# Attention and routed experts on one core: k'q's sixth step of batch 1 in routing step 5, a step's squares between slot 0's casts and joins, step 3's scatters behind slot 0's rows

## The chip, the cores and the metric

The kernel runs on one core of one Trainium2 chip. The metric is the device time of one execution in microseconds (us); for the kernel before it is the median of three runs. The profile is of one more execution, taken by the hardware profiler.

## What is computed

Channel attention over four batches, and a mixture of experts on its output. Cut to what matters:

```python
B, N, C = 4, 5056, 256                      # q, k, v: [B, N, C] float32
qn = q / (norm(q, axis=1) + 1e-6)           # norms over the N tokens
kn = k / (norm(k, axis=1) + 1e-6)
a  = softmax(kn^T @ qn / tau)               # per batch [C, C]
x  = (v @ a).reshape(20224, 256)
logits = x @ w_gate + modality_bias[modality_id]     # 8 experts
e = argmax(logits); g = softmax(logits)[e]
out[t] = g[t] * (relu(x[t] @ w1[e]) @ w2[e])         # w1: 256x1024, w2: 1024x256
```

## The kernel before

**Steps.** Tokens are taken 512 at a time: ten steps per batch, the last one short. Three kinds of work run over such steps.

- *k'q* (`kq_pieces(b, s)`): q and k of the step are loaded (L302), their product is added to the 256x256 matrix `g` of the batch on TensorE (L365), and their squares are added to `acc` for the norms: ScalarE squares (`sq`, L344), VectorE adds (L346), two halves of two squares and two adds a step. In batch 0, and in the first six steps of batch 1 (indices 0 to 5, `WHOLE`), the float32 values go to TensorE as they are; later steps are split into a high and a low part first (`qs`, `ks`: ScalarE cast L320, VectorE subtraction L321). Squares can be put off: with a list `later` they are run when the text reaches that list.
- *Routing* (`va_pieces`, `g` counts the steps 0 to 39 over all batches): v of the step is transposed, split into `vh` and `vl` (L571, L572), multiplied by the attention matrix (`xp`, L585), copied to `x` (L592 to L597) with the gate's logits beside it (`L`, L598), and every token gets a row number. GpSimd then scatters the 512 rows to `xs` in DRAM by four indirect DMAs (`send`, L474). For steps 0 to 5 v is transposed by TensorE (`vtp`); from step 6 on by a transposing DMA (`T`, L534) and a second one that takes the half-words apart (`pl`, L511), whose parts ScalarE and VectorE join again (`vt`, L518, L519).
- *Blocks* (`block_pieces`): a slot is a block of 512 rows of one expert. `load_x` fetches its rows with a transposing DMA (`Tx`, L766) and its weights and tokens (`gt`, L769); `load_w` fetches w1 and w2 in halves (`w1r`, `w2r`, L788, L792); `split_w` casts them and subtracts (L811, L818); `tr_x` joins the rows (`xt`, L518, L519) and splits them (`xh`, `xl`, L830, L831); `m1` and `m2` are the two matrix products (`hp` L845, `y` L866) with relu and its low part between them (`hh` L848, `hl` L849); `finish` and `store` scale the result and scatter it to the output.

**Order.** Batch 0's k'q runs first, alone. Then the routing steps follow one another, and the pieces of a step are interleaved with those of a block and with k'q steps of the next batch. `first_block` is 6: slot 0 is computed in routing step 6. It is chosen after step 2 and needs the rows of steps 0 to 2; slot 1 needs step 3's too. `PLAN` says which k'q steps of batch 1 run beside which routing step; `product` makes the pieces of such a task, `ask` issues its load, `products_of` puts both in order. `squares` holds squares put off to the end of a step.

The text is not the order on the engines. A planner takes the instructions of each engine's queue by priority (the place in the text) and by its own estimate of when they are ready, so an instruction can run ahead of its place. `order(ins, others)` keeps an instruction behind others on the same queue without a wait; `after(ins, others)` is a true wait. Each queue then runs strictly in its order. All loads are issued on SyncE's queue (SP), all scatters on GpSimd's (POOL).

`HELD` names routing steps whose scatters are not sent at once: those of steps 3 and 4 were sent in the next step, behind its fourth copy. `turned` is slot 0's `tr_x`, called at the end of step 5 with the instructions behind which its joins are kept, before the change the last cast and subtraction of `split_w` (`evicted[-1]`).

Buffers that matter: `q` and `k` have two each, which indices 0, 1 and 4 onwards of batch 1 use in turn; indices 2 and 3 use the three of `w1r` and `w2r`, which slot 0's weights need next; the `x` of steps 1 and 3 use the two of `Tx`.

Of the kernel before, what the change touches and what calls it, by code (L numbers as in the profile page):

```python
# [13 lines left out]
AF = mybir.ActivationFunctionType  # L14
ALU = mybir.AluOpType
# [20 lines left out]
def kernel(  # L36
# [13 lines left out]
    nc = tc.nc  # L50
    P = 128
    B, N, C = q.shape
# [4 lines left out]
    NS = -(-N // STEP)  # L57
# [19 lines left out]
    START = 2  # L77

    BEFORE = [0, 1]
    PLAN = [[], [2], [], [3], [4], [], [5], [], [6, 7], [8, 9]]  # L80
    AHEAD = 4

    SKIP = (12,)

    first_block = LAG + START

    HELD = {3: 3, 4: 3}

    def parts(s):
        return P if s < NS - 1 else PL  # L90
# [82 lines left out]
    pads = []  # L173
    asked = []
    turning = []
    written = [[] for _ in range(G)]

    def pad_rows():
# [87 lines left out]

    gram = {}
    filled = []
    acc = {}

    def kq_pieces(b, s, behind=(), later=None):

        pp = parts(s)
        st = {}
        t0 = s * STEP

        def act(ins):
            order(ins.ins, [i for n, i in (behind() if callable(behind) else behind) if n == "act"])

        def dve(ins):  # L280
            order(ins.ins, [i for n, i in (behind() if callable(behind) else behind) if n == "dve"])

        def begin():
            if s == 0:
                gram[b] = ps1.tile([P, CH, C], F32, tag="y0" if b == 0 else "g", name=f"g_{b}")
                acc[b] = p1.tile([P, 2, 2 * C], F32, tag="acc", name=f"acc_{b}", bufs=2)
                if b == 0:
                    p1.tile([P, 48], F32, tag="filler2", name="filler2")

        def load():  # L290
            if b == 0:
                begin()
            for n, src, tag in (("q", q, "w1r"), ("k", k, "w2r")):
                if (b == 0 and s % 5 >= 2) or (b == 1 and 2 <= s < START + 2):
                    st[n] = p3.tile([P, TT, C], F32, tag=tag, name=f"{n}_{b}_{s}")
                else:
                    st[n] = p2.tile([P, TT, C], F32, tag=n, name=f"{n}_{b}_{s}")
                rows = src[b, t0 : t0 + pp * TT, :].rearrange("(p t) c -> p t c", t=TT)
                if b == 0 and s == 0:
                    st[n + "rows"] = rows  # L300
                else:
                    nc.sync.dma_start(st[n][:pp], rows)  # L302
            if b == 0 and s == 0:
                for h in range(2):
                    ts = slice(2 * h, 2 * h + 2)
                    for n in ("q", "k"):
                        nc.sync.dma_start(st[n][:, ts, :], st[n + "rows"][:, ts, :])

        def split(h):
            if b > 0 and h == 0:  # L310
                begin()
            ts = slice(2 * h, 2 * h + 2)
            whole = s in WHOLE[b]
            more = h == 1 and (b == 0 or (b == 1 and s < START + 1))
            if not whole:
                st["q", h] = p2.tile([P, 2, 2 * C], F32R, tag="xh" if more else "qs", name=f"qs_{b}_{s}_{h}")
                st["k", h] = p2.tile([P, 2, 2 * C], F32R, tag="xl" if more else "ks", name=f"ks_{b}_{s}_{h}")
            for n in () if whole else ("q", "k"):
                t = st[n, h]
                act(nc.scalar.copy(t[:pp, :, 0:C], st[n][:pp, ts, :]))  # L320
                dve(nc.vector.tensor_tensor(  # L321
                    t[:pp, :, C : 2 * C], st[n][:pp, ts, :], t[:pp, :, 0:C].bitcast(F32), ALU.subtract
                ))
            if later is None:
                square(h)
            else:
                later.append(lambda: square(h))

        def square(h):
            ts = slice(2 * h, 2 * h + 2)  # L330
            a = acc[b]
            for n, o in (("q", 0), ("k", C)):
                first = h == 0 and s == 0
                sq = a[:, :, o : o + C]
                if not first:
                    if b == 0 and s == 0 and n == "q":
                        p3.tile([P, 80], F32, tag="filler5", name="filler5", bufs=1)
                    if b == 0 and n == "k" and not filled:
                        filled.append(p3.tile([P, 48], F32, tag="filler1", name="filler1", bufs=1))
                    if b == 0 or (b == 1 and s < AHEAD):  # L340
                        sq = p3.tile([P, 2, C], F32, tag="hh" if n == "q" else "hl", name=f"sq_{b}_{s}_{h}_{n}")
                    else:
                        sq = p3.tile([P, 2, C], F32, tag="vt", name=f"sq_{b}_{s}_{h}_{n}")
                act(nc.scalar.activation(sq[:pp], st[n][:pp, ts, :], AF.Square))  # L344
                if not first:
                    dve(nc.vector.tensor_tensor(a[:pp, :, o : o + C], a[:pp, :, o : o + C], sq[:pp], ALU.add))  # L346

        def mm(h):
            for t in range(2):
                first = s == 0 and h == 0 and t == 0  # L350
                last = s == NS - 1 and h == 1 and t == 1
                for m in range(CH):
                    ms = slice(m * P, (m + 1) * P)
                    if s in WHOLE[b]:
                        seq = [(st["k"][:pp, 2 * h + t, ms], st["q"][:pp, 2 * h + t, :])]
                    else:
                        ks, qs = st["k", h], st["q", h]
                        lo = slice(C + m * P, C + (m + 1) * P)
                        seq = [
                            (ks[:pp, t, ms], qs[:pp, t, 0:C]),  # L360
                            (ks[:pp, t, ms], qs[:pp, t, C : 2 * C]),
                            (ks[:pp, t, lo], qs[:pp, t, 0:C]),
                        ]
                    for i, (x, y) in enumerate(seq):
                        nc.tensor.matmul(  # L365
                            gram[b][:, m, :], x, y, start=first and m == 0 and i == 0,
                            stop=last and i == len(seq) - 1, skip_group_check=True,
                        )

        yield load  # L370
        for h in range(2):
            yield lambda h=h: split(h)
            yield lambda h=h: mm(h)
# [97 lines left out]
    routed = {}  # L471
# [24 lines left out]
    def lag(g):  # L496

        n = LAG
        for x in SKIP:
            n -= g >= x + n  # L500
        return n
# [245 lines left out]
    def block_pieces(g, slot, picked, tail):  # L747
        pki, padded = picked
        st = {"wr": {}, "wc": {}, "h": {}}
# [11 lines left out]
        def load_x():  # L761
# [3 lines left out]
            for ins in (  # L765
# [10 lines left out]
                        ins.ins, group=f"x{later}", reason="the block's rows were all there when it was taken"  # L776
                    )
                tc.add_to_no_dep_group("xr", ins.ins)
                if slot == 1:
                    turning.append(ins.ins)  # L780

        def load_w(hf):
            if hf == 0:
# [142 lines left out]
    def run(pieces):  # L926
        for f in pieces:
            f()
# [48 lines left out]
    def product(n):  # L977
        g, b, i = tasks[n]
        if n not in products:
            products[n] = list(kq_pieces(  # L980
                b, i, (lambda: routed.get(g, routed[g - 1])) if b == 1 else (),
                squares.setdefault(g + (3 if g + 2 == first_block else 1), [])
                if b == 1 and (g < first_block or i == NS - 1) else None,
            ))
        return products[n]
# [3 lines left out]
    def ask(n):  # L989
        if n < len(tasks) and n not in loaded:  # L990
            loaded.add(n)
            product(n)[0]()

    def products_of(g):

        out = []
        for n, (at, b, i) in enumerate(tasks):
            if at == g:
                out += [lambda n=n: ask(n)] if g <= first_block else []
                out += product(n)[1:]  # L1000
                if g >= first_block and (b, i) != (1, NS - 1):
                    out.append(lambda n=n: ask(n + (1 if g == first_block else 2)))
        if g == first_block + 1:
            out.append(lambda: ask(min(n for n in range(len(tasks)) if tasks[n][0] > g) + 1))
        return out

    va = [va_pieces(*divmod(g, NS)) for g in range(G)]
# [9 lines left out]
    for g in range(G):  # L1017
# [12 lines left out]
            done.add((0, "prep"))  # L1030
            begun = [split0, split1]
        own = list(va[g][1])
        if g - 1 in HELD:
            t = HELD[g - 1]
            own.insert(t + 1, lambda: va[g - 1][4]([copied[g, t]]))
        turn = []
        if g + 1 < first_block:
            turn.append(va[g + 1][2])
# [13 lines left out]
        if b + 1 < B:  # L1052
            if b == 0 and s == 1:
                streams.append(list(kq_pieces(1, 2, lambda: routed[1], squares[2])))
            else:
                streams.append(products_of(g))
        _interleave(*streams)
        if waiting and waiting[0][0] <= g + 1 - lag(g + 1):
            blk = waiting[0][1]
            once(blk, "load")  # L1060
            if blk["slot"] == 0:
                turned(blk["evicted"][-1])
            once(blk, "prep")
        if s == NS // 2 + 2 and b < B - 1:
            setup_bias(b + 1, routed[g])
# [91 lines left out]
```

## Time and profile before

| | |
|---|---|
| median of 3 runs | 1173.28 us (1173.11 to 1174.34) |
| the profiled execution: time, span | 1176.94 us, 1175.1 us |
| granted TensorE clock | 0.998 |
| busy: TensorE, weight loads, VectorE, ScalarE, GpSimd | 1152.9, 1054.9, 919.4, 806.5, 386.9 us |
| DMA | 228.38 MB, mean 194 GB/s |

The span runs from the first to the last instruction. PE is TensorE's matmuls, PEld its weight loads, DVE VectorE, ACT ScalarE, POOL GpSimd, SP SyncE (SPq its queue of DMA issues). A row of a timeline has the start and the duration in us, the engine, the line, the operation and out<-in by the names of the tiles without their numbers; the bracket at the end is the idle time of that engine just before it, and what ended it. Where a merged row has x2 or more, the duration covers all of them. Rows of one engine can overlap a little, since instructions are pipelined.

### The profile page before, as it was taken

What the parts mean: (1) busy time and instruction counts of PE and PEld (TensorE: products, weight loads), DVE (VectorE), ACT (ScalarE), POOL (GpSimd) and SP (SyncE); (2) the same over time, 40 slices, a digit from 0 to 9 for tenths busy, and PEclk for the clock granted to TensorE, in tenths of its full rate; (3) what the DMA queues carried; (4) which work ended last, traced back from release to release, by engine and by line L of the source; (5) the groups of instructions that cost most, each with busy time, mean ns of one, the idle gap of its engine ahead of it and who ended that gap; (6) DMA issues with size and microseconds to landing.
All of it is one profiled execution on the core that took longest, in us unless ns stands there. A gap on an engine that the chain in (4) does not pass through costs nothing.

```text
span 1175.1 us, 23436 instructions
## 1 busy us (share of the span) xinstructions
PE 1152.9 (98%) x7748; PEld 1054.9 (90%) x7748; DVE 919.4 (78%) x2590; ACT 806.5 (69%) x1655; POOL 386.9 (33%) x345
## 2 busy tenths in 40 slices
PE   8997999999999999999999999999999999999997
PEld 7886889999999999999999999999999999999997
DVE  6787889898788888888888888878767776685552
ACT  6676877877777777687776777767666666555552
POOL 0054334323333333333333333333333333344122
PEclk9999999999999999999999999999999999999999
DMA  8969999689777677758777766665875665565420
GB/s 311 295 223 235 274 234 261 175 238 218 199 202 198 196 197 207 202 166 228 211 204 209 207 197 165 169 175 162 218 202 174 190 173 156 143 170 144 127 91 30
DMA packets 285843, 228.38 MB, mean 194 GB/s; under 512 B 185064, under 2 KB 243944, under 8 KB 285712
## 3 DMA queue, kind: packets, MB, share of 16 engines
q1 hardware_dynamic: 270032, 185.19, 60.0%
q0 software_dynamic: 15680, 41.61, 10.3%
q8 instruction: 62, 1.02, 0.4%
q14 instruction: 69, 0.57, 0.2%
HBM read 128.79 MB, written 43.43 MB: 147 GB/s over the span
## 4 chain that ended last, share of the span: by engine, by line
PE 84%; issue 7%; DVE 3%; DMA 2%; POOL 2%; ACT 1%; SPq 0%; POOLq 0%; ACTq 0%; DVEq 0%
PE y L866 32%; PE hp L845 32%; PE g L365 10%; PE xp L585 9%; POOL out_dram L474 2%; DMA pl<-T 1%; DMA Tx<-xs 1%; DVE hl L849 0%; DMA xs<-x,pi 0%; DVE inv L398 0%; PE vtp L567 0%; PE gw L434 0%; DVE w2l L818 0%; SPq L511 0%; DMA k<-in_k_dram 0%
## 5 line engine op out<-in xcount | busy, mean ns | idle before, releaser
L866 PE MATMUL y<-w2h,hh 128*128 128x256 f32 x1256 | 354.5, 282 | 0.0
L866 PE MATMUL y<-w2l,hh 128*128 128x256 f32 x1256 | 351.2, 280 | 0.0
L866 PE MATMUL y<-w2h,hl 128*128 128x256 f32 x1256 | 349.5, 278 | 0.1
L474 POOL DMA_INDIRECT xs<-x,pi x160 | 199.1, 1245 | 362.8 <-DVE pr L708 182.8
L474 POOL DMA_INDIRECT out_dram<-yo,gt x158 | 175.2, 1109 | 391.6 <-ACT hh L848 296.8
L845 PE MATMUL hp<-xh,w1h 128*128 128x512 f32 (+1 forms) x640 | 250.0, 391 | 6.1 <-ACT xh L830 3.5
L845 PE MATMUL hp<-xl,w1h 128*128 128x512 f32 (+1 forms) x640 | 250.1, 391 | 0.0
L845 PE MATMUL hp<-xh,w1l 128*128 128x512 f32 (+1 forms) x640 | 248.8, 389 | 0.0
L866 PEld LDWEIGHTS y<-w2h,hh 128*128 128x128 f32 x1256 | 236.4, 188 | 9.5 <-issue 0.2
L866 PEld LDWEIGHTS y<-w2l,hh 128*128 128x128 f32 x1256 | 236.4, 188 | 8.4
L849 DVE SCALAR_TENSOR_TENSOR hl<-hp,hh 128x512 fp32r<-128x512 f32 (+1 forms) x320 | 217.0, 678 | 34.3 <-ACT hh L848 30.8
L866 PEld LDWEIGHTS y<-w2h,hl 128*128 128x128 f32 x1256 | 235.3, 187 | 0.4 <-DVE hl L849 0.3
L848 ACT ACTIVATE hh<-hp 128x512 fp32r<-128x512 f32 (+1 forms) x320 | 188.7, 590 | 59.9 <-PE hp L845 58.7
L811 ACT CAST w1h<-w1r 128x512 fp32r<-128x512 f32 x160 | 99.3, 621 | 169.5 <-PE hp L845 141.2
L818 DVE TENSOR_TENSOR w1l<-w1r,w1h 128x512 fp32r<-128x512 f32 x160 | 110.0, 687 | 90.6 <-ACT w1h L811 87.3
L845 PEld LDWEIGHTS hp<-xh,w1l 128*128 128x128 f32 x640 | 120.1, 188 | 25.8
L845 PEld LDWEIGHTS hp<-xh,w1h 128*128 128x128 f32 x640 | 119.9, 188 | 20.3 <-ACT xh L830 3.7
L845 PEld LDWEIGHTS hp<-xl,w1h 128*128 128x128 f32 x640 | 120.2, 188 | 13.7 <-DVE xl L831 0.4
L818 DVE TENSOR_TENSOR w2l<-w2r,w2h 128x512 fp32r<-128x512 f32 x160 | 109.9, 687 | 12.0 <-ACT w2h L811 9.3
L811 ACT CAST w2h<-w2r 128x512 fp32r<-128x512 f32 x160 | 100.3, 627 | 20.3 <-PE y L866 18.4
L597 DVE COPY x<-xp 128x256 uint16<-128x256 uint16 x136 | 57.1, 420 | 52.3 <-ACT x L596 50.7
L585 PE MATMUL xp<-ah,vh 128*128 128x264 f32 x320 | 92.6, 291 | 1.2 <-DVE L L598 1.2
(162 smaller groups left out, 1827.6 us busy)
## 6 DMA issues: line engine op xcount, KB each, us to landing
w1r<-in_moe_w_dram SPq DMA_DIRECT2D x80, 512.0 KB
w2r<-in_moe_w_dram SPq DMA_DIRECT2D x80, 512.0 KB
q<-in_q_dram SPq DMA_DIRECT2D x35, 512.0 KB
k<-in_k_dram SPq DMA_DIRECT2D x35, 512.0 KB
pl<-T SPq DMA_DIRECT2D x120, 128.0 KB
v<-in_v_dram SPq DMA_DIRECT2D x6, 512.0 KB
xs<-x,pi POOLq DMA_INDIRECT x160
out_dram<-yo,gt POOLq DMA_INDIRECT x158
```

The source lines that it names most:

```text
L365: nc.tensor.matmul(gram[b][:, m, :], x, y, start=first and m == 0 and i == 0, stop=last and i == len(seq) - 1, skip_group_check=True,)
L474: ins = nc.gpsimd.indirect_dma_start(out=dst, out_offset=bass.IndirectOffsetOnAxis(ap=idx, axis=0), in_=rows, in_offset=None, bounds_check ...
L585: nc.tensor.matmul(xp[:, 0:DE], a[:, h, t * P : (t + 1) * P], w[:, h, :], start=i == 0, stop=i == len(seq) - 1,)
L597: copied[g, t] = nc.vector.tensor_copy(planes[:, 0, :], halfwords[:, 0, :]).ins
L811: ins = nc.scalar.copy(hi, src).ins
L818: evicted[-1] = [ins, nc.vector.tensor_tensor(lo, src, hi.bitcast(F32), ALU.subtract).ins]
L845: nc.tensor.matmul(hp[:, 0:rows], w[:, h, fs], x[:, h, 0:rows], start=i == 0, stop=i == len(seq) - 1)
L848: relu = nc.scalar.activation(hh[:, 0:rows], hp[:, 0:rows], AF.Relu).ins
L849: low = nc.vector.scalar_tensor_tensor(hl[:, 0:rows], hp[:, 0:rows], 0.0, hh[:, 0:rows].bitcast(F32), ALU.max, ALU.subtract).ins
L866: ins = nc.tensor.matmul(y, a[:, tsl], w[:, j % 2, :], start=(j == 0 and i == 0 and t % per == 0), stop=(j == NJ - 1 and i == 2), skip_gro ...
```

## The change

It edits the plan of batch 1's k'q steps and the place of three kinds of work around slot 0.

- `PLAN`: index 5 (the sixth step) is written in routing step 5 instead of 6, index 6 in step 7 instead of 8; index 7 stays in step 8.
- Squares: those of index 3 are run at the end of step 5, after slot 0's casts (`gap`) and before its joins, which are kept behind the last of them (`newest`); before, they ran at the end of step 3. Those of index 5 join those of index 4 at the end of step 6.
- Scatters: step 3's are sent in step 5 and wait for both of slot 0's row loads (`rows_in`); before, they were sent in step 4 behind its fourth copy.
- `products_of`: the loads of the k'q tasks are asked for in another order; index 5's in step 4.

```diff
--- before.py
+++ after.py
@@ -77,14 +77,14 @@
     START = 2
 
     BEFORE = [0, 1]
-    PLAN = [[], [2], [], [3], [4], [], [5], [], [6, 7], [8, 9]]
+    PLAN = [[], [2], [], [3], [4], [5], [], [6], [7], [8, 9]]
     AHEAD = 4
 
     SKIP = (12,)
 
     first_block = LAG + START
 
-    HELD = {3: 3, 4: 3}
+    HELD = {3: None, 4: 3}
 
     def parts(s):
         return P if s < NS - 1 else PL
@@ -173,6 +173,7 @@
     pads = []
     asked = []
     turning = []
+    rows_in = []
     written = [[] for _ in range(G)]
 
     def pad_rows():
@@ -266,6 +267,8 @@
 
     gram = {}
     filled = []
+    newest = []
+    gap = []
     acc = {}
 
     def kq_pieces(b, s, behind=(), later=None):
@@ -341,9 +344,12 @@
                         sq = p3.tile([P, 2, C], F32, tag="hh" if n == "q" else "hl", name=f"sq_{b}_{s}_{h}_{n}")
                     else:
                         sq = p3.tile([P, 2, C], F32, tag="vt", name=f"sq_{b}_{s}_{h}_{n}")
-                act(nc.scalar.activation(sq[:pp], st[n][:pp, ts, :], AF.Square))
+                squared = nc.scalar.activation(sq[:pp], st[n][:pp, ts, :], AF.Square)
+                act(squared)
                 if not first:
-                    dve(nc.vector.tensor_tensor(a[:pp, :, o : o + C], a[:pp, :, o : o + C], sq[:pp], ALU.add))
+                    added = nc.vector.tensor_tensor(a[:pp, :, o : o + C], a[:pp, :, o : o + C], sq[:pp], ALU.add)
+                    dve(added)
+                    newest[:] = [squared.ins, added.ins]
 
         def mm(h):
             for t in range(2):
@@ -776,8 +782,8 @@
                         ins.ins, group=f"x{later}", reason="the block's rows were all there when it was taken"
                     )
                 tc.add_to_no_dep_group("xr", ins.ins)
-                if slot == 1:
-                    turning.append(ins.ins)
+                if slot < 2:
+                    (rows_in, turning)[slot].append(ins.ins)
 
         def load_w(hf):
             if hf == 0:
@@ -978,8 +984,8 @@
         g, b, i = tasks[n]
         if n not in products:
             products[n] = list(kq_pieces(
-                b, i, (lambda: routed.get(g, routed[g - 1])) if b == 1 else (),
-                squares.setdefault(g + (3 if g + 2 == first_block else 1), [])
+                b, i, (lambda: gap if g + 3 == first_block else routed.get(g, routed[g - 1])) if b == 1 else (),
+                squares.setdefault({3: 6, 4: 7, 5: 7}.get(g, g + 1), [])
                 if b == 1 and (g < first_block or i == NS - 1) else None,
             ))
         return products[n]
@@ -994,14 +1000,17 @@
     def products_of(g):
 
         out = []
-        for n, (at, b, i) in enumerate(tasks):
-            if at == g:
-                out += [lambda n=n: ask(n)] if g <= first_block else []
-                out += product(n)[1:]
-                if g >= first_block and (b, i) != (1, NS - 1):
-                    out.append(lambda n=n: ask(n + (1 if g == first_block else 2)))
-        if g == first_block + 1:
-            out.append(lambda: ask(min(n for n in range(len(tasks)) if tasks[n][0] > g) + 1))
+        mine = [n for n, task in enumerate(tasks) if task[0] == g]
+        if g <= first_block + 1:
+            out += [lambda n=n: ask(n) for n in mine]
+        if g + 2 == first_block:
+            out += [lambda n=n: ask(n + 1) for n in mine]
+        for n in mine:
+            out += product(n)[1:]
+            if g == first_block + 1:
+                out.append(lambda n=n: ask(n + 1))
+            if g > first_block and tasks[n][1:] != (1, NS - 1):
+                out.append(lambda n=n: ask(n + 2))
         return out
 
     va = [va_pieces(*divmod(g, NS)) for g in range(G)]
@@ -1030,9 +1039,11 @@
             done.add((0, "prep"))
             begun = [split0, split1]
         own = list(va[g][1])
-        if g - 1 in HELD:
+        if HELD.get(g - 1) is not None:
             t = HELD[g - 1]
             own.insert(t + 1, lambda: va[g - 1][4]([copied[g, t]]))
+        if g + 1 == first_block:
+            own.insert(0, lambda: va[g - 2][4](rows_in))
         turn = []
         if g + 1 < first_block:
             turn.append(va[g + 1][2])
@@ -1055,11 +1066,14 @@
             else:
                 streams.append(products_of(g))
         _interleave(*streams)
+        if g + 1 == first_block:
+            gap += list(zip(("act", "dve"), waiting[0][1]["evicted"][-1]))
+            run(squares.pop(first_block))
         if waiting and waiting[0][0] <= g + 1 - lag(g + 1):
             blk = waiting[0][1]
             once(blk, "load")
             if blk["slot"] == 0:
-                turned(blk["evicted"][-1])
+                turned(newest)
             once(blk, "prep")
         if s == NS // 2 + 2 and b < B - 1:
             setup_bias(b + 1, routed[g])
```

## The prediction

> **What bounds the kernel now.** I read the page first (busy shares, slices, queues), then the busy time of each engine in stretches of 10 us, then the chain that ended last, then each engine's instructions in order of time from 75 to 165 us.
>
> ```profile
> span 1175.1 us, 23436 instructions
> ...
> PE 1152.9 (98%) x7748; PEld 1054.9 (90%) x7748; DVE 919.4 (78%) x2590; ACT 806.5 (69%) x1655; POOL 386.9 (33%) x345
> ...
> q0 software_dynamic: 15680, 41.61, 10.3%
> ```
> PE is busy for 1152.9 of 1175.1 us, so all its gaps together are 22.2 us, and the change moves no matmul in or out. It can gain only by closing gaps, and lose only by opening others. The stretches of 10 us show where they are:
>
> ```profile
> 90.00:100.00 10.00, 6.54 (x41) 5.28 (x39) 6.46 (x39) 4.87 (x13) 5.11 (x6) 1.00 1.17 249
> 100.00:110.00 10.00, 10.00 (x68) 9.14 (x67) 6.33 (x27) 6.43 (x14) 5.91 (x6) 1.00 0.94 261
> 110.00:120.00 10.00, 7.52 (x44) 6.17 (x42) 8.92 (x25) 7.81 (x18) 0.00 (x0) 1.00 1.22 205
> 120.00:130.00 10.00, 9.96 (x72) 9.13 (x72) 9.73 (x35) 8.90 (x18) 3.05 (x3) 1.00 1.03 297
> 130.00:140.00 10.00, 10.00 (x65) 9.08 (x64) 10.00 (x29) 8.26 (x20) 4.15 (x5) 1.00 1.16 249
> 140.00:150.00 10.00, 10.00 (x69) 8.97 (x69) 6.02 (x18) 6.95 (x13) 2.10 (x2) 1.00 1.07 329
> 150.00:160.00 10.00, 8.02 (x55) 6.96 (x54) 10.00 (x29) 7.49 (x17) 6.33 (x4) 1.00 1.11 191
> ```
> The columns are PE, PEld, DVE, ACT, POOL, granted clock (1.00 throughout), DMA share and GB/s. PE loses 3.46 us in 90 to 100, 2.48 in 110 to 120 and 1.98 in 150 to 160. PE's own rows give the releasers, in brackets behind the idle time:
>
> ```profile
> 86.63 0.39 PE L585 MATMUL xp<-ah,vh 128*128 128x264 f32 x1 [1.16 <-DVE L L598]
> ...
> 87.47 3.19 PE L365 MATMUL g<-q,k 128*128 128x256 f32 x14
> ...
> 96.89 0.73 PE L845 MATMUL hp<-xh,w1h 128*128 128x512 f32 x2 [3.46 <-ACT xh L830]
> ...
> 111.92 0.50 PE L845 MATMUL hp<-xh,w1h 128*128 128x512 f32 x1 [1.72 <-DVE hl L849]
> ...
> 115.73 0.50 PE L845 MATMUL hp<-xh,w1h 128*128 128x512 f32 x1 [0.76 <-DVE hl L849]
> ...
> 156.25 0.38 PE L365 MATMUL g<-qs,ks 128*128 128x256 f32 x1 [1.08 <-DVE qs L321]
> ```
> The first block's first matmul is the one at 96.89. The chain says what it waited for, and what is late 10 us after:
>
> ```profile
> 82.05 5.37 DMA xs<-x,pi
> ...
> 88.14 6.34 DMA Tx<-xs
> ...
> 104.17 3.48 DMA pl<-T
> ```
> Routing step 2's last scatter lands at 87.4, then slot 0's rows take 6.34 us and land at 94.5; the joins and the cast xh follow in 2.4 us. The 111.92 gap hangs on pl, the next v planes, which land at 107.65.
>
> **The change, part by part.**
>
> *The sixth k'q step (index 5) written in routing step 5.* Its matmuls are where the text now asks for them already. The tile query on g shows it:
>
> ```profile
> L365 PE MATMUL g<-q,k x256: 377/379/765, 4.6 to 90.8; 128*128 128x256 f32 x120, 112*128 112x256 f32 x8
> ```
> The unsplit steps are ten of batch 0 and six of batch 1; 256 records over 16 steps are 16 each, so the sixth of batch 1 is the group at 87.47 and ends near 91. The planner had hoisted it out of step 6, its load too. The move of the matmuls and of the load's request I therefore cost at 0; bounds: -3.2 us (that group's 3.19 us, were it now to fill the 3.46 gap) and +3.2 (were it to fall between slot 0's first matmuls).
>
> *Its squares go to the end of step 6.* They sit now in the worst place:
>
> ```profile
> 107.73 0.77 ACT L518 COPY vt<-pl 128x512 uint16<-128x512 uint16 x1 [1.60 <-DMA pl<-T]
> 108.37 0.62 ACT L344 ACTIVATE sq_q<-q 128x512 f32<-128x512 f32 x1
> ...
> 109.42 0.60 ACT L811 CAST w1h<-w1r 128x512 fp32r<-128x512 f32 x1
> ...
> 110.45 0.59 ACT L848 ACTIVATE hh<-hp 128x512 fp32r<-128x512 f32 x1
> ...
> 109.02 0.69 DVE L346 TENSOR_TENSOR acc<-acc,sq_q 128x512 f32<-128x512 f32 x1 [1.44 <-ACT sq_q L344]
> ```
> The two squares hold ACT from 108.37 to 109.42, 1.05 us, between the late vt copy and the hh that PE's 111.92 matmul needs through hl. Without them hh, hl and that matmul come 1.05 us earlier; DVE's two adds (from 109.02) finish before hl's turn and cost nothing more. The later pair on ACT is at 111.70, where DVE's backlog and not ACT sets the 0.76 gap: 0 for it. All four adds (4 x 0.60 = 2.4 us of DVE) must run elsewhere; DVE is idle for 3.67 of 100 to 110, so that is the cover, and without it they go into 120 to 140, where DVE is 97 to 100% busy. Term: -1.05, bounds -2.48 (both gaps) and 0.
>
> *The fourth step's squares (index 3) go between slot 0's casts and its joins; the joins are tied behind them.*
>
> ```profile
> 84.02 0.67 DVE L346 TENSOR_TENSOR acc<-acc,sq_q 128x512 f32<-128x512 f32 x1
> ...
> 85.83 0.67 DVE L346 TENSOR_TENSOR acc<-acc,sq_k 128x512 f32<-128x512 f32 x1
> ...
> 89.51 1.06 ACT L592 COPY x<-xp 128x512 uint16<-128x512 uint16 x2
> ...
> 94.50 0.45 DVE L519 COPY xt<-Tx 128x512 uint16<-128x512 uint16 x1 [2.36 <-DMA Tx<-xs]
> ```
> The four adds at 84.02 to 86.43 go, and with them the 1.16 gap, but PE then only reaches the wait for xh sooner. DVE now works without a pause from 84.02 to 92.14 and then idles 2.36; the same work in another order ends at 92.14 or, where the last square lands late, about 93.3: ACT is done with its casts and x copies at 90.57, four squares of 0.52 make it 92.65, and the last add of 0.60 follows. So the joins can start at 93.3, 1.2 before 94.5. The new order costs nothing as long as the rows land later than that.
>
> *Step 3's scatters wait for slot 0's rows.*
>
> ```profile
> 85.15 2.21 POOL L474 DMA_INDIRECT xs<-x,pi  x1 [2.06 <-ACT x L592]
> ...
> 91.94 0.98 POOL L474 DMA_INDIRECT xs<-x,pi  x1 [0.30 <-issue]
> ...
> 96.59 0.98 POOL L474 DMA_INDIRECT xs<-x,pi  x1 [3.67 <-ACT x L592]
> ...
> 106.80 3.30 SPq L766 DMA_TRANSPOSE Tx<-xs  x1
> ...
> 1047.60 2.09 SPq L766 DMA_TRANSPOSE Tx<-xs  x1
> ...
> 1051.00:1052.00 1.00, 1.00 (x10) 0.99 (x9) 0.86 (x7) 0.48 (x1) 0.00 (x0) 1.00 0.09 12
> ```
> The four run from 85.15 to 92.9, across the rows' 88.14 to 94.5. Queue q0's 10.3% of the span over 318 scatters (160 + 158) is 0.38 us of all sixteen DMA engines each, so four are 1.5 us. Late in the kernel a row load issued at 1047.60 with little beside it is over by 1051.0: 3.4 us. So the rows land between 91.5 (alone) and 94.5 (no change); 94.5 - 1.5 = 93.0 is my value, so the joins' 93.3 binds: slot 0's first matmul at 95.7, -1.2 us. Queued behind the new wait on POOL are step 4's scatters (now 96.59) and step 5's: four at 1.28 us from about 93.5 end at 98.6, so those slip by 2 us. Slot 1's rows (106.80 on SP) need step 3's scatters landed; 98.6 plus the 5.37 us that a landing took is 104.0: 0, with 2.8 us to spare. Two of the four formerly ran before the rows' data did, so some 0.75 us of transfers now meets the v fetch and pl; but pushing step 4's back takes about as much away. Term for pl: 0, bounds -1.5 and +1.5.
>
> [...]
>
> *The 1.2 us do not last.* PE starting earlier runs dry earlier, at 109.0 instead of 110.2 (111.92 less 1.72), and the next matmul waits for pl all the same. What is carried past 112 is the -1.05 alone.
>
> *The seventh step (index 6) goes from step 8 to step 7.* Now its DVE work starts at
>
> ```profile
> 155.53 0.67 DVE L321 TENSOR_TENSOR qs<-q,qs 128x512 fp32r<-128x512 f32 x1
> ...
> 160.74 0.67 DVE L346 TENSOR_TENSOR acc<-acc,sq_k 128x512 f32<-128x512 f32 x1
> ```
> eight instructions at 0.60 = 4.8 us, in the stretch where DVE is at 10.00 and PE loses 1.98. In step 7 (126 to 150) DVE has 4.25 idle of the 30 us from 120 to 150, nearly all past 140. I take the gap in 150 to 160 as closed: -1.98; bounds -1.98 and +0.6 (4.8 - 4.25 as a new stall, the gap staying). Its load now comes after the squares of indices 4 and 5, which free its buffers. The next two steps' loads are asked for in step 7 as well; with two buffers for each of q and k, the squares before them decide when they go: 0.
>
> **Sum.** -1.05 - 1.98 + 0 = -3.0 us. The profiled execution took 1176.94 us (span 1175.1), 3.66 above the median 1173.28; 1173.9 for it, 1170.3 as a median.
>
> **The rivals.**
> 1. *Everything is carried through*: rows land alone (-2.9), both gaps after 110 close (-2.48), and 150 to 160 closes (-1.98): -7.4, 1165.9. For it: the clean 3.4 us. Against: the joins' 93.3 and pl at 107.65, which nothing here advances.
> 2. *DVE is the bound in step 7*: index 5's squares bring 2.4 us and index 6 brings 4.8 between 117 and 150, where DVE is full until 140. A stall of 2.4 + 4.8 - 4.25 = 2.95 replaces the gains: -0.1, 1173.2. For it: 9.73 and 10.00 in the stretches. Against: the idle 3.67 before 110.
> 3. *The scatters hit the v fetch*: pl at +1.5, so -1.5, 1171.8; with the gap in 150 to 160 only half closed, 1172.7. For it: DMA shares of 0.94 to 1.22 from 90 to 130. Against: step 4's scatters, pushed back by as much. [...]
> 4. *Slower, by SP's queue.* The seventh step's load is now
>
> ```profile
> 118.99 0.52 SPq L302 DMA_DIRECT2D q<-in_q_dram  x1
> ...
> 120.92 2.59 SPq L511 DMA_DIRECT2D pl<-T  x4
> ...
> 125.48 0.63 ACT L344 ACTIVATE sq_k<-k 128x512 f32<-128x512 f32 x1 [0.33 <-DVE acc L346]
> ```
> ahead of the next pl on SP. Its buffers come free only with the late squares, the last of which ends at 126.1. If it keeps its place, SP stands for up to 7.1 us, pl and the vt copies are that late, PE stalls about 6: +3, 1176.3. It decides from some 5 us of standing on. Against: the load is written after those squares.
>
> **How the numbers follow.** No change, here, is within 0.2% or 2.35 us. Forecast (-5 to -1.5) 0.36, of it 0.30 past -2.35; rival 1 0.12; rival 2 0.20, of it 0.03 faster; rival 3 0.14; rival 4 0.18. Faster 0.30 + 0.12 + 0.03 = 0.45, same 0.06 + 0.17 + 0.14 = 0.37, slower 0.18. The range reaches to rivals 1 and 4: 1166.0 to 1176.0; the forecast's own is 1168.3 to 1171.8.
>
> **What would show it.** No scatters between 85 and 92, four from about 93.5; the xt joins near 93.3 with DVE busy up to them; slot 0's first matmul near 95.7; no squares between vt and hh near 108, and the gap there starting earlier and ending near 110.9; qs before 150 and no PE wait for qs after. It is wrong if the rows still take 6 us, if PE waits for hl in 126 to 150, or if SP stands before pl near 120.

## The result and the profile after

The changed kernel takes 1185.69 us (median of 4 runs, 1184.15 to 1186.2); the kernel before, beside it on the same chip, 1173.81 us: ratio 1.0092, 95% interval 1.0073 to 1.0111. On another chip it was 1.0068 [1.0044, 1.0093]. It is slower by 8 to 12 us, outside the forecast's range. The profiled execution took 1186.2 us. In the experiments below two executions took 2938 and 2307 us; the ratios leave them out, and of the kernel whose profiled one was the second (index 5's squares late, alone) only the times are used.

```profile
span 1184.4 us, 23437 instructions
...
PE 1156.1 (98%) x7748; PEld 1058.0 (89%) x7748; DVE 920.8 (78%) x2590; ACT 807.1 (68%) x1655; POOL 382.5 (32%) x345
```
The span is 9.3 us longer. PE's gaps sum to 28.3 us instead of 22.2, so 6.1 of the 9.3 are idle time. The other 3.2 are busy time, 1156.1 against 1152.9 with the same 7748 matmuls: some ran slower (the 128x512 products `hp` of 144.76 to 146.04 took 0.63 us each, those of 150.26 to 151.42 took 0.39). PE's gaps, each with its releaser:

```profile
76.14 0.39 PE L591 MATMUL xp<-ah,vh 128*128 128x264 f32 x1 [1.55 <-DVE L L604]
...
92.02 0.19 PE L647 MATMUL rp<-oh,trim 128*128 128x32 bf16 x1 [2.37 <-DVE oh L622]
...
100.17 0.73 PE L851 MATMUL hp<-xh,w1h 128*128 128x512 f32 x2
...
112.24 0.50 PE L851 MATMUL hp<-xh,w1h 128*128 128x512 f32 x1 [1.96 <-DVE hl L855]
...
144.16 0.80 PE L371 MATMUL g<-qs,ks 128*128 128x256 f32 x2 [7.98 <-ACT ks L323]
```
The one at 144.16 is new and by far the largest. The one at 76.14 is new too. Slot 0's first product comes at 100.17, 3.3 us later than before. ScalarE's and SyncE's rows name the cause of the large gap:

```profile
128.76 0.62 ACT L347 ACTIVATE sq_k<-k 128x512 f32<-128x512 f32 x1
...
141.00 0.62 ACT L323 CAST qs<-q 128x512 fp32r<-128x512 f32 x1 [7.82 <-DMA q<-in_q_dram]
...
131.78 4.39 SPq L772 DMA_TRANSPOSE Tx<-xs  x1
...
136.92 0.43 SPq L305 DMA_DIRECT2D q<-in_q_dram  x1
```
The row at 128.76 is the last of the eight squares put off, those of indices 4 and 5. The load of index 6 is asked for at 136.92, behind slot 2's rows (131.78) on SP; before, it was asked for at 118.99. ScalarE stands 7.82 us at its first cast, with slot 1's next relu behind it. In the kernel before, the same cast came earlier and waited for nothing:

```profile
133.88 0.62 ACT L320 CAST qs<-q 128x512 fp32r<-128x512 f32 x1
```
By stretches (PE, PEld, DVE, ACT, POOL, granted clock, DMA share, GB/s):

```profile
130.00:140.00 10.00, 6.18 (x44) 5.47 (x43) 5.80 (x18) 3.18 (x9) 4.03 (x3) 0.95 1.16 273
140.00:150.00 10.00, 5.84 (x26) 5.45 (x27) 6.69 (x13) 7.52 (x14) 1.95 (x2) 0.54 0.86 311
150.00:160.00 10.00, 10.00 (x70) 9.24 (x69) 8.22 (x24) 8.72 (x18) 2.43 (x2) 1.00 1.08 211
```
The gap in 150 to 160 has closed, as forecast; one of 7.98 us stands 15 us earlier, and the mean granted clock is 0.54 in 140 to 150. The start of slot 0 has its own rows:

```profile
59.82 0.33 SPq L305 DMA_DIRECT2D q<-in_q_dram  x1
...
65.44 0.33 SPq L536 DMA_DIRECT2D v<-in_v_dram  x1
65.87 0.37 SPq L305 DMA_DIRECT2D k<-in_k_dram  x1
66.30 3.11 SPq L517 DMA_DIRECT2D pl<-T  x4
...
84.24 0.42 SPq L794 DMA_DIRECT2D w1r<-in_moe_w_dram  x1
...
91.03 2.52 SPq L772 DMA_TRANSPOSE Tx<-xs  x1
...
74.99 0.45 DVE L525 COPY vt<-pl 128x512 uint16<-128x512 uint16 x1 [3.19 <-DMA pl<-T]
...
89.56 1.14 ACT L817 CAST w1h<-w1r 128x512 fp32r<-128x512 f32 x2 [2.15 <-DMA w1r<-in_moe_w_dram]
...
98.26 0.67 DVE L350 TENSOR_TENSOR acc<-acc,sq_k 128x512 f32<-128x512 f32 x1
98.96 0.44 DVE L525 COPY xt<-Tx 128x512 uint16<-128x512 uint16 x1
...
85.73 0.97 POOL L480 DMA_INDIRECT xs<-x,pi  x1 [0.39 <-ACT x L598]
...
89.58 0.98 POOL L480 DMA_INDIRECT xs<-x,pi  x1 [0.30 <-issue]
```
In the kernel before, SP had

```profile
59.85 1.40 SPq L511 DMA_DIRECT2D pl<-T  x2
...
65.74 1.26 SPq L511 DMA_DIRECT2D pl<-T  x2
67.10 0.56 SPq L302 DMA_DIRECT2D q<-in_q_dram  x1
```
There index 5's load (67.10) stood behind all four transfers of pl. Now it stands ahead of them, q at 59.82 and k at 65.87, and a v fetch with it; VectorE waits 3.19 us for pl. Slot 0's weights are asked for at 84.24 (80.94 before), so casts, squares, adds and joins follow one another to 98.96. And step 3's scatters run at 85.73 to 90.6, about where they ran before (from 85.15) and ahead of the rows' issue at 91.03: the new wait is not there. The kernel's text gives a reason: the rows' load and the scatters declare themselves independent of each other (group `x3` in `load_x`, group `xr` in `scatter`'s call). The run below that takes these declarations out shows that they had cancelled the written dependence.

### The profile page after: what moved, and what is told of

It is laid out like the page before. It is cut to its first block, busy times and chain, and to the rows that moved or that the text cites. A ratio compares the mean times of both kernels' runs of the same rounds, so it can differ in the third digit from the quotient of the medians.

```text
span 1184.4 us, 23437 instructions
## 1 busy us (share of the span) xinstructions
PE 1156.1 (98%) x7748; PEld 1058.0 (89%) x7748; DVE 920.8 (78%) x2590; ACT 807.1 (68%) x1655; POOL 382.5 (32%) x345
## 4 chain that ended last, share of the span: by engine, by line
PE 85%; issue 6%; DMA 4%; POOL 1%; ACT 1%; DVE 1%; SPq 1%; POOLq 0%; ACTq 0%; DVEq 0%
PE y L872 33%; PE hp L851 32%; PE g L371 9%; PE xp L591 9%; POOL out_dram L480 1%; DMA pl<-T 1%; DMA k<-in_k_dram 1%; DMA T<-in_v_dram 1%; DMA w2r<-in_moe_w_dram 1%; DMA xs<-x,pi 1%; PE gw L440 0%; PE vtp L573 0%; DVE vl L578 0%; SPq L517 0%; ACT w2h L817 0%
## 5 line engine op out<-in xcount | busy, mean ns | idle before, releaser
L480 POOL DMA_INDIRECT xs<-x,pi x160 | 196.0, 1225 | 363.4 <-DVE pr L714 189.9
```

The lines of the kernel that those rows point to most:

```text
L480: ins = nc.gpsimd.indirect_dma_start(out=dst, out_offset=bass.IndirectOffsetOnAxis(ap=idx, axis=0), in_=rows, in_offset=None, bounds_check ...
```

## The experiments

Ratios are to the kernel before on the same chip in the same series, with 95% intervals. The first theory, after the traces: the loads' places on SP are the loss, index 6's above all. Rivals: VectorE is the bound in step 7; the order around slot 0 is the loss; the scatters are.

**Index 6 back in step 8** (changed kernel).
```diff
-PLAN = [[], [2], [], [3], [4], [5], [], [6], [7], [8, 9]]
+PLAN = [[], [2], [], [3], [4], [5], [], [], [6, 7], [8, 9]]
+if g in (first_block, first_block + 1):
+    out.append(lambda: ask(g - 3))
```
(The added lines ask for the loads of indices 6 and 7 in steps 6 and 7.)


> Changed kernel, but k'q's seventh step (index 6) is back in routing step 8, and its load is asked for in step 6; all else stays. Theory L (the load of index 6 came too late, TensorE waited 7.98 us for it from 136.2 to 144.2, and the clock then stood at half until 149.1): both go, the 2 us gap near 155 comes back, 1176 to 1179 us. Rival P (the loss is made before 110 us, where slot 0's first product came about 4 us late, and the later wait only takes the place of waits that come anyway): 1183 to 1186.

Measured 1.0014 [1.0000, 1.0028]. The wait near 140 is gone, and with it most of the loss, though index 5's early load is still there.

**Index 6's load asked for in step 6** (changed kernel, index 6 in step 7).
```diff
+if g == first_block:
+    out.append(lambda: ask(3))
```


> Changed kernel with one more line: the load of index 6 is asked for in step 6, its work stays in step 7. Theory L: SyncE issues it ahead of slot 2's rows, the 7.98 us wait shrinks under 1.5 us and the half clock goes, 1175 to 1178.5. Rival D (the work of index 6 does not fit into step 7, ScalarE and VectorE are full there): TensorE waits there all the same, 1182 to 1186. Rival B (the two buffers of q and k come free only with the squares put off to the end of step 6): the load stands in SyncE's queue until about 128 and holds the v fetch and slot 2's rows behind it, 1179 to 1183.

Measured 1.0043 [1.0026, 1.0060]. The load goes out at 125.48, with index 4's late squares just done, and the wait shrinks but stays:

```profile
131.38 0.62 ACT L323 CAST qs<-q 128x512 fp32r<-128x512 f32 x1 [2.24 <-DMA q<-in_q_dram]
...
134.09 0.38 PE L371 MATMUL g<-qs,ks 128*128 128x256 f32 x1 [2.42 <-ACT ks L323]
```

**Index 5's load back behind pl** (changed kernel).
```diff
-if g + 2 == first_block:
-    out += [lambda n=n: ask(n + 1) for n in mine]
```


> Changed kernel, but index 5's load is asked for in step 5 and not in step 4. Theory P (in the changed kernel q of index 5 and the v of step 5 stand ahead of step 6's planes pl in SyncE's queue, VectorE waits 3.19 us for them at 71.8 and TensorE 1.55 us, the clock falls to half from 77.2 to 80.5): these go, slot 0's weights are asked for 3 us sooner, 1181.5 to 1184. Rival (hidden by the waits for the planes of step 7 and for index 6): 1185 to 1187.

Measured 1.0058 [1.0039, 1.0077]. The gap at 75 is gone, but another stood before slot 0:

```profile
89.27 0.62 ACT L577 CAST vh<-vt 128x512 fp32r<-128x512 f32 x1 [5.23 <-remote]
...
93.95 0.21 PE L647 MATMUL rp<-oh,trim 128*128 128x32 bf16 x1 [7.03 <-DVE oh L622]
```
The trace names no releaser for ScalarE's 5.23 us. Such unnamed waits of 3 to 5 us were in the profiles of all four kernels of this first series, between 81 and 91, and in neither of the changed kernel's own two. What caused them stays open; so the ratios of this series bound the parts, and later series check them.

**Index 3's squares back in their old place** (changed kernel).
```diff
-squares.setdefault({3: 6, 4: 7, 5: 7}.get(g, g + 1), [])
+squares.setdefault({4: 7, 5: 7}.get(g, g + 1), [])
```
(the squares' `gap` goes too, and the joins are tied to the casts again)


> Changed kernel, but index 3's squares are back at the end of step 3 and slot 0's joins behind its last cast. Theory Q (the adds end at 98.9 and hold the joins, the rows were there by 95): first product of slot 0 2 to 3 us earlier, 1183 to 1184.5 since the planes at 110 take part of it back. Rival (the joins waited for the weights' casts and the rows anyway, the squares filled idle time): 1185 to 1187.

Measured 1.0060 [1.0042, 1.0078]; first product at 98.93, and ScalarE's wait for q still 5.49 us. A small part at most.

**The changed kernel again, and with the wait made true.** In the second, `load_x` of slot 0 no longer declares itself independent of step 3's scatters, nor they of it.
```diff
-for later in range(g + 1, G):
+for later in range(g + (2 if slot == 0 else 1), G):
-xs[:, :], ..., ["x", "xr"], ["x", f"x{g}"], ...
+xs[:, :], ..., ["x"] if behind is rows_in else ["x", "xr"], ["x", f"x{g}"], ...
```


> The changed kernel itself, on the chip of the three runs beside it, so that they can be set against it. All theories: 1.007 to 1.011 of before, a PE gap of about 8 us ending near 144 on qs, and slot 0's first product near 100.

> The changed kernel, with step 3's scatters held by a true wait for slot 0's rows (the changed kernel's own scatters went at 85.73, ahead of the rows' issue at 91.03). The instructions of every queue are in the order of the changed kernel. Theory of the loads' places: four scatters behind 95, the rows' flight shorter than 6 us, but the joins still held by index 3's adds until 98.9, so slot 0's first product stays within 1 us of 100.17, and the time within 2 us of the changed kernel's. Rival, the scatters are what costs (they run beside slot 0's weights): weights land 1.5 to 2 us earlier, the first product comes near 98 and the time falls by 2 us or more. As the prediction had it, in the changed kernel's favour: -1.2 us at the first product, not carried on.

Measured 1.0068 [1.0044, 1.0093] and 1.0085 [1.0058, 1.0113]: no gain. With the true wait, step 3's scatters start at

```profile
96.71 1.23 POOL L480 DMA_INDIRECT xs<-x,pi  x1 [12.10 <-DVE lm L612]
```
and the tile view of its Tx says of slot 0's rows (asked for at 89.94, so landed at 95.7):
```profile
DMA to landing us min/median/max: 5.8/5.8/5.8
```
In the changed kernel's run beside it, with the scatters ahead of the rows, the chain has
```profile
90.54 6.74 DMA Tx<-xs
```
Without any scatter beside them the rows still take 5.8 us, not 3.4: against 6.34 in the kernel before and 6.74 here, the scatters are worth 0.5 to 0.9 us to them. What fills the rest is not shown.

**Two parts of the change alone, then together, on the kernel before.** Index 5's squares late:
```diff
-if b == 1 and (g < first_block or i == NS - 1) else None,
+if b == 1 and (g <= first_block or i == NS - 1) else None,
```


> The kernel before with one part of the change: index 5's squares put off to the end of routing step 6. The prediction's term: -1.05 us, the gap before the matmul of 111.92 shorter by that. Queue theory: the squares hold q and k of index 5 for longer, so index 6's load goes behind three more requests on SP; index 6 runs in step 8 here and has the time, so 0 to -1 us: ratio 0.999 to 1.000. Rival (VectorE is short after 120): the four adds come in 120 to 140 where it is full, +1 to +2.4 us.

Index 6 in step 7:
```diff
-PLAN = [[], [2], [], [3], [4], [], [5], [], [6, 7], [8, 9]]
+PLAN = [[], [2], [], [3], [4], [], [5], [6], [7], [8, 9]]
-out.append(lambda n=n: ask(n + (1 if g == first_block else 2)))
+out.append(lambda n=n: ask(n + (1 if g in (first_block, first_block + 1) else 2)))
```


> The kernel before with one part of the change: index 6 in routing step 7, its load where it was on SP (issued near 119), index 5's squares not put off. Theory of the loads' places: no gap of 8 us near 140, since q and k are there by 126; the 1.98 us in 150 to 160 go or stay, so -2 to +1 us, ratio 0.998 to 1.001. Rival (VectorE is the bound in step 7, +4.8 us of work there): a stall of 2 to 3 us or more in 126 to 150, on hl or qs from VectorE, ratio 1.002 to 1.004. If the move itself, not its load, made the loss, a gap near 8 us would be here too: ratio 1.007.

Both edits:


> The kernel before with two parts of the change together: index 5's squares put off to the end of step 6 and index 6 in step 7. Alone, the first gave 1.000 [0.9985, 1.0016] and the second 1.0029 [1.0016, 1.0041]. Buffer theory: index 6's load takes the buffers of index 5, which are now held until the late squares (about 126 to 129), so its load goes out some 8 us later than 118.99, ScalarE stands at qs until about 133, and a gap of 2 to 5 us opens on qs or ks in 128 to 140 that neither part alone has: ratio 1.005 to 1.008. Rival (the parts simply add, VectorE's work being the price): 1.003, and no such gap.

Measured 1.0000 [0.9985, 1.0016], 1.0029 [1.0016, 1.0041] and 1.0051 [1.0035, 1.0067]. In the second, whose rows come first, index 6's load goes out on time, and it is index 7's that comes late. That ratio is the one that the rival (VectorE) forecast, and the gap at 144.58 is on hl, as it said; but behind it stands ScalarE, 6.16 us without q, and VectorE is idle from 141 to 143. Then the rows with both edits:

```profile
116.25 0.52 SPq L302 DMA_DIRECT2D q<-in_q_dram  x1
...
137.94 0.49 SPq L302 DMA_DIRECT2D q<-in_q_dram  x1
...
142.17 0.62 ACT L320 CAST qs<-q 128x512 fp32r<-128x512 f32 x1 [6.16 <-DMA q<-in_q_dram]
...
144.58 0.50 PE L845 MATMUL hp<-xh,w1h 128*128 128x512 f32 x1 [2.56 <-DVE hl L849]
```
```profile
130.42 0.50 SPq L302 DMA_DIRECT2D q<-in_q_dram  x1
...
136.10 0.62 ACT L320 CAST qs<-q 128x512 fp32r<-128x512 f32 x1 [4.69 <-DMA q<-in_q_dram]
...
138.43 0.58 PE L365 MATMUL g<-qs,ks 128*128 128x256 f32 x1 [4.83 <-ACT ks L320]
```
The gap of 4.83 us is in neither part alone. It was forecast from the order of ScalarE's queue: before, index 5's squares run ahead of index 4's (they start at 108.37), and index 6's load, at 118.99, goes out before index 4's, so it takes index 5's buffers. Put off, index 5's squares follow index 4's, and both pairs of buffers are held until late in step 6. No row names the buffer; the gap came as this account had it. VectorE is at 5.63 of 10 us in 130 to 140 there: not the bound.

**Index 5 in step 5, its load in step 4, alone on the kernel before** (its squares run with it, and before slot 0's product in the trace).
```diff
-PLAN = [[], [2], [], [3], [4], [], [5], [], [6, 7], [8, 9]]
+PLAN = [[], [2], [], [3], [4], [5], [], [], [6, 7], [8, 9]]
...
-if b == 1 and (g < first_block or i == NS - 1) else None,
+if b == 1 and (g < first_block and i != 5 or i == NS - 1) else None,
...
+if g + 2 == first_block:
+    out += [lambda n=n: ask(n + 1) for n in mine]
...
```


> The kernel before with index 5 in step 5 and its load asked for in step 4, its squares at the end of step 5, all else as before. Queue theory: the load of q and k of index 5 and v stand ahead of all four pl of step 6 on SP, pl is late by 5 us, a gap of 1 to 1.6 us near 75 and the half clock behind it, slot 0's weights asked for 1 to 3 us later: +2 to +5 us, ratio 1.002 to 1.004. As predicted (the planner had hoisted it all): 0, ratio 1.000.

Measured 1.0052 [1.0035, 1.0069], more than expected.

```profile
60.74 0.37 SPq L302 DMA_DIRECT2D q<-in_q_dram  x1
...
67.02 3.15 SPq L511 DMA_DIRECT2D pl<-T  x4
...
110.56 1.38 ACT L518 COPY vt<-pl 128x512 uint16<-128x512 uint16 x2 [9.44 <-DMA pl<-T]
...
100.56 0.19 PE L641 MATMUL rp<-oh,trim 128*128 128x32 bf16 x1 [4.39 <-DVE oh L616]
...
112.44 0.58 PE L866 MATMUL y<-w2h,hh 128*128 128x256 f32 x1 [6.87 <-ACT hh L848]
```
All four pl requests stand behind index 5's load, slot 0 starts at 100.6, and the next pl lands near 110.5. ScalarE stands 9.44 us at its vt copies with the hh that slot 0 needs behind them, and PE loses 6.87 us there. The load's place is the changed kernel's, but the squares' is not, and the gaps sit elsewhere than there (1.96 us at 112.24): the order of the queues around slot 0 differs. So this ratio is not the move's price in the changed kernel.

**Index 3's squares alone, and what is left without the moves.** Alone on the kernel before, twice; with index 5's late squares; the changed kernel without the two moves; and that without index 3's squares too.

> The kernel before with index 3's squares between slot 0's casts and joins, all else as before. As predicted: VectorE's adds end by 93.3 and the rows land at 94.5, so 0. Theory after the runs: with slot 0's weights asked for at 81 the casts end near 89, the squares near 93 and the adds near 94, so still 0 to +1 us at slot 0's first product (96.89), ratio 1.000 to 1.001; the cost in the changed kernel then came from the weights' being late. Rival (the order itself is the cost): the joins held until 96 or later, first product past 98.5, ratio 1.002 or more.

> The kernel before with index 3's squares between slot 0's casts and joins alone, as before 0.9983 [0.9972, 0.9993]: faster than both kernels if that holds, 0.997 to 0.9995. Rival (chance): 1.000 or above.

> The kernel before with both edits of the squares (index 3's in the gap, index 5's at the end of step 6) and none of the moves. If they add: 0.998 (0.997 to 0.9995). Rival (index 5's late squares delay the late ones of index 4 and with them slot 1): 1.000 or more.

> The changed kernel with only the two costly moves undone: index 6 back in step 8, and index 5's load asked for in step 5 again. Index 3's squares stay between slot 0's casts and joins, index 5's squares stay late, the scatters stay. If the parts add (index 3's squares alone gave 0.9983, the late squares of index 5 alone 1.000): 0.998 to 1.000, no wait of ScalarE for q near 140, no gap at 75. Rival (the order around slot 0 costs in itself once index 5 is written in step 5, as the 7.03 us gap before slot 0 suggested when only its load was put back): 1.002 or more, with a wait before slot 0 longer than the 3.46 us of before.

> The changed kernel with three parts undone: index 6 back in step 8, index 5's load asked for in step 5 again, index 3's squares back at the end of step 3's routing order. What is left is index 5 written in step 5, its late squares, and the scatters' place. If the loads' places and the squares are the whole loss: 1.000 (0.9985 to 1.0015), no gap but those of the kernel before, granted clock 0.995 to 0.998. Rival (the rest costs too, the scatters or the sixth step's place): 1.002 or more.

Measured: index 3's squares alone 0.9983 [0.9972, 0.9993], then 0.9994 [0.9983, 1.0004]: a gain of 1 us perhaps, not settled, though slot 0's first product comes at 98.61 and 98.93, 1.7 and 2.0 us later than before. Both squares 1.0002 [0.9988, 1.0016]. The changed kernel with index 6 back in step 8 and index 5's load back in step 5: 1.0009 [0.9996, 1.0022]; without index 3's squares too, 1.0013 [0.9999, 1.0027]. The 0.998 that was expected of both squares, and the gain with the moves undone, did not show. The loss goes with the moves, and nearly all of it with index 6's alone: moving that one back gave 1.0014, and undoing index 5's early load as well gave 1.0009, which the intervals do not tell apart.

## Why the prediction was wrong

*The seventh step from step 8 to 7, taken at -1.98.* This is the step that failed. "Its load now comes after the squares of indices 4 and 5, which free its buffers" stood there as a cost of nothing. The gap in 150 to 160 did close, but the load went out 18 us later than before, ScalarE stood 7.82 us at the first cast, and PE lost 7.98 us, with the clock at 0.50 from 139.0 to 149.2. The kernel before already ran this step's four casts in step 7 (from 133.88), and the term counted VectorE's work alone. With the step back in 8 and its load asked for in step 6, the ratio is 1.0014, where the changed kernel has 1.0068 to 1.0092.

Two delays make up the 18 us. The late squares hold the buffers, but the last of them ends at 129.4, 7.5 us before the request, and asked for in step 6 the load goes out at 125.48 already. The rest, some 7.5 to 11.4 us, is the request's place: the edit writes it in step 7, behind slot 2's rows, where the kernel before wrote it in step 6. The prediction let the squares decide when the load goes, and put nothing down for its place on the queue. Asking in step 6 alone brought the ratio to 1.0043. Rival 4 had the buffers and a stall of about the right size (6 us), but the wrong place, and +3 us where 8 to 12 were measured: SP did not stand at this load, ScalarE stood behind it.

*The squares of index 5, taken at -1.05.* The gap was to end at 110.9 and ended at 112.24, for pl was later still:

```profile
110.25 0.76 ACT L524 COPY vt<-pl 128x512 uint16<-128x512 uint16 x1 [4.60 <-DMA pl<-T]
```
That is 2.5 us after 107.73, past the bound of 1.5 set for pl. The mechanism itself held, at twice its size: from this copy to the matmul it is 1.99 us, where it was 4.19 with the squares between. Alone, on the kernel before, the late squares moved nothing (1.0000). Their place was called the worst, but it let index 6 have its buffers early; together with the move above they cost a gap of 4.83 us.

*The sixth step, taken at 0.* Its matmuls had indeed run that early, and its load too (67.10), but behind pl; the edit puts one q, one v and one k ahead of pl. The bounds of 3.2 us were those of the matmuls; the load had none. Alone, with its squares ahead of slot 0's product, the move cost 0.52%, some 6 us. In the changed kernel it cost less: taking the early load out of it gave 1.0058, 0.10 to 0.34% below its 1.0068 to 1.0092, and with index 6 back in step 8 it made no difference clear of the noise.

*The scatters.* The edit did nothing on the chip, which was no rival of mine. Nor was the premise right: made true, the wait gave the rows 5.8 us where 3.4 was the clean figure. No run shows rival 3's 1.5 us on pl. What the true wait moved, in one pair of profiles: the rows land 0.9 us sooner after their request (5.8 against 6.74), and ScalarE's copy behind the next pl comes at 111.31 instead of 110.84, 0.5 us later; the time did not fall (1.0085 against 1.0068).

*Index 3's squares, at 0 as long as the rows land later than 93.3.* Right alone. In the changed kernel the weights came 3.3 us later, the casts and the squares with them, and the adds held VectorE's joins until 98.96. The rows were there by 97.31, when ScalarE began its own joins, so the condition no longer held.

*Rival 2, VectorE the bound in step 7,* is refuted: in the stretch where the gap of 8 us begins, VectorE was at 5.80 of 10.

The parts, each alone on the kernel before, sum to about the whole: the sixth step 0.52%, the seventh with the late squares 0.51%, index 3's squares -0.17 or -0.06%, so 0.86 to 0.97%, against 0.68 and 0.92% measured. That they add so well is chance: their gaps sit in other places when they act together, and the sixth step's 0.52% is not what it costs there.

## What to carry to other kernels

When a step is moved, follow its load: which buffers it takes, what frees them, and what stands ahead of the request on its queue. Work that seems to sit in the worst place may be what frees a buffer; look up who waits for that before moving it. A written dependence counts only if the trace shows the wait.

## What was not expected of the hardware

The granted clock fell to half behind gaps, and not by their length alone. In the changed kernel, stretches of 1 us (same columns):

```profile
77.00:78.00 1.00, 1.00 (x8) 0.76 (x6) 0.93 (x9) 0.73 (x2) 0.00 (x0) 0.76 0.00 0
...
80.00:81.00 1.00, 1.00 (x6) 1.00 (x6) 0.74 (x3) 0.83 (x3) 0.52 (x1) 0.54 0.00 0
...
139.00:140.00 1.00, 0.00 (x0) 0.00 (x0) 0.00 (x0) 0.00 (x0) 0.00 (x0) 0.50 1.03 307
...
149.00:150.00 1.00, 1.00 (x10) 1.00 (x9) 1.00 (x3) 0.52 (x1) 0.00 (x0) 0.90 0.84 258
```
The gap of 1.55 us before 76.14 was followed by half clock for 3.4 us, from 77.5 to 80.9 by the means 0.76 and 0.54 of its first and last stretch; the 3.46 us of the kernel before, at 96.89, by none (1.00 in 90 to 100 and in 100 to 110). At the gap of 7.98 the clock stood at 0.50 from 139.0 to 149.2, three times as long and 5 us into the work that followed. In five experiments the means of the stretches of 10 us from 130 to 160 add up to this much half clock: 3.4 us with index 5's squares late and index 6 in step 7 on the kernel before (0.92, 0.91, 1.00; gap 4.83), 3.6 with index 6's load asked for in step 6 (0.83, 0.99, 1.00; gap 2.42), 6.8 with index 3's squares back (1.00, 0.66, 1.00; gap 5.85), 10.2 in the changed kernel again (1.00, 0.51, 0.98; gap 6.74) and with the wait made true (1.00, 0.66, 0.83; gap 8.34). What set off the spell behind the 1.55 us stays open: in the changed kernel again, a gap of 1.26 us at 76.32 was followed by 1.00 in 77 to 78 and in 80 to 81. Over six runs of the changed kernel again the mean granted clock was 0.991 to 0.993, over the 21 of the kernel before beside them 0.995 to 0.998. Of the 9.3 us between the two profiles 3.2 are PE's longer busy time, so here the gaps priced by their length alone would be priced too low.
